# Attention and two feed-forward layers on one core: the first batch's values summed by TensorE, the second batch's queries and keys summed by GpSimd

## The chip, the cores and the metric

The kernel runs on one core of a Trainium2 chip. The metric is device time in microseconds (us) of one execution. TensorE is PE in the rows below (PEld its weight loads), VectorE is DVE, ScalarE is ACT, GpSimd is POOL, and SyncE is SP, which issues most of the DMAs.

## The reference

Four batches, eight heads, 576 tokens, 64 numbers per head. Two attentions are added: one over tokens averaged by fours (the pooled one, 144 queries and keys), its result repeated four times, and one over a narrow band of each token's neighbours (the local one). The 2304 tokens of 512 numbers that come out pass through two feed-forward layers, each 512 to 2048 to 512.

```python
def reference_core(q, k, v, w_in, w_out, w2_in, w2_out):
    q_d, k_d, v_d = (x.reshape(B, H, S // 4, 4, D).mean(axis=3) for x in (q, k, v))
    out_up = np.repeat(sm_attn(q_d, k_d, v_d), 4, axis=2)
    mask = np.abs(pos[:, None] - pos[None, :]) < 4
    scores = np.where(mask, scale * np.matmul(q, k.transpose(0, 1, 3, 2)), -1e9)
    out_local = np.matmul(softmax(scores), v)
    x = (out_up + out_local).transpose(0, 2, 1, 3).reshape(B * S, H * D)
    h = np.maximum(x @ w_in, 0.0)
    x = h * h @ w_out
    h = x @ w2_in
    g = np.maximum(h, 0.0) + np.log1p(np.exp(-np.abs(h)))
    return g @ w2_out
```

## The kernel before

**Order.** The program is written out by a planner. Each piece of work is a Python generator that yields the engine it wants, an assumed duration and what it needs; `Order.run` always takes the piece that could start first (ties by urgency) and only then emits its instructions. The planner's assumptions (for DMA those of `landed`) thus fix the order in which every engine runs its instructions; on the chip each engine works through its own list and waits in place for what is late.

**Feed-forward.** The tokens stand in five blocks of 512, 384, 512, 512 and 384 (`BLOCKS`). A step is one block times one of 16 slices of a layer: `hidden` makes `ph` with 12 products (each f32 product is split in a high and a low part, three products for each of four slices of the input), `activate` turns it into `gh` and `gl` on ScalarE and VectorE, and `outputs` adds 12 (or 9) products to `y`. The first two slices of the first block are done in halves of 256 tokens, so the first step needs only four of the eight local blocks (`half_ready`). Weights come as 64-bit numbers in half slices of 512 KB (`load_weights`, tile `raw`, three buffers) and are split on ScalarE and VectorE (`weight_job`: `f`, `r`, `w`).

**Attention of the first two blocks.** `pooled` handles one pair of heads: it sums queries and keys by fours (`qkd`), multiplies them (`psc`), takes the softmax (`pn`, `pe`), transposes it (`ppp`, copied to `ppt`), sums the values by fours (`vd`) and multiplies (`ppo`, copied to `up`). `local` handles 64 tokens: `lsc`, softmax in `le`, transpose `lpp`, copied to `lpt`, product with the values `lav`, to which `up` is added in `lt`; then the high part `xh` and the low part `xl` are the input of the feed-forward layer. For batch 0 VectorE makes both sums by fours; for batch 1 (`SUMS_ON_PE`) TensorE sums queries and keys with four products by the identity (`pqk`), and ScalarE copies the sum. Where TensorE's list would leave it idle before the fifth step, `keep_busy` puts in a product by the identity, `idle`, whose result nobody reads. The first pair tiles are lent from the weight slots and are called `w_first` in the rows; those of the values are called `first`.

**Loads.** SyncE's list goes, at the start, through identity, batch 0's queries and keys, its values (`pv`, 72 rows of 4 KB each), the mask, the local values (`lv`, 70 rows), the first two pairs of batch 1, and then the first weights.

Of the kernel before, what the change touches and what calls it, by code (L numbers as in the profile page):

```python
# [9 lines left out]
F32 = mybir.dt.float32  # L10
# [62 lines left out]
SUMS_ON_PE = [1]  # L73
# [17 lines left out]
CROWDED = 25.0  # L91
# [108 lines left out]
class Order:  # L200
# [85 lines left out]
def fused_kernel(ctx: ExitStack, tc: tile.TileContext, lq, lk, lv, dqk, dv, cdmask, pqk, pv, wts, cmask, cident, out):  # L286
# [13 lines left out]
    ident = const.tile([128, 128], F32, name="ident")  # L300
    mask = const.tile([128, 3, KW], F32, name="mask")
# [17 lines left out]
    r_pt = ring(att, "pt", [KH, 2 * 288], BUFS["pt"])  # L319
# [59 lines left out]
    more_slots = Event()  # L379
# [99 lines left out]
    lent, first_bufs = {}, {}  # L479

    def lend():

        for p in range(LENT):
            k = SLOTS1 - 1 - p
            lent[k] = Host()
            both = wpool.tile([128, 2048], F32, name=f"w_first{k}", tag=f"w{k}")
            if p < NP:
                first_bufs["in", p] = Guest(both[:, :2 * QKW], lent[k])
                first_bufs["in", p].left = 1 + BLOCKS[0]
                s0 = 2 * QKW  # L490
                first_bufs["qkd", p] = Guest(both[:, s0:s0 + 2 * SP], lent[k])
# [4 lines left out]
        for p, r in enumerate((r_xh[1], r_xl[1])):  # L496
            b = r.take("first")
            host = Host(b)
            x = b.tile.bitcast(F32).rearrange("p h n -> p (h n)")
            for two in range(2):  # L500
                first_bufs["pv", 2 * p + two] = Guest(x[:KH, two * 1024:two * 1024 + 1024], host)
# [26 lines left out]
    def load_tasks():  # L528
# [3 lines left out]
        order.landed(t, 65536)  # L532
# [5 lines left out]
        for (kind, at, hp, i, _), ev in zip(tasks, arrived, strict=True):  # L538
            if kind == "d":
                continue  # L540
            if kind == "l" and not i:
                if at % 2 == 0:
                    t = yield "sp", 0.06, *room(r_v, "v", at // 2)
                    bv = take_for(r_v, "v", at // 2)
                    bv.left = 2
                    sp.dma_start(out=bv.tile[:KW], in_=lv[at // 2])
                    vthere = order.landed(t, KW * 4096)
                ev.buf = None, None, bv, at % 2
                ev.at = 0.0
                ev.v.at = vthere  # L550
            elif kind == "l":
                if at % 2 == 0:
                    two = at // 2
                    t = yield "sp", 0.06, *room(r_q, "q", two), *room(r_k, "k", two), *room(r_v, "v", two)
                    bq, bk, bv = (take_for(r, x, two) for r, x in ((r_q, "q"), (r_k, "k"), (r_v, "v")))
                    for x in (bq, bk, bv):
                        x.left = 2
                    sp.dma_start(out=bq.tile, in_=lq[at // 2])
                    order.landed(t, 256 << 10)
# [5 lines left out]
                    vthere = order.landed(t, KW * 4096)  # L565
                ev.buf = bq, bk, bv, at % 2
                ev.at = there
                ev.v.at = vthere
            else:
                for x, two in [(ev, at * NP + hp)] + [(ev.next, at * NP + hp + 1)] * (at in BY_TWOS):  # L570
                    if at:
                        t = yield "sp", 0.06, r_in
                        x.buf = r_in.take("in")
                        sp.dma_start(out=x.buf.tile, in_=pqk[two])
                        x.at = order.landed(t, 128 * 8 * QKW)
                    late = i in DIRECT
# [4 lines left out]
                    x.v.at = order.landed(t, KH * 4096)  # L581
# [18 lines left out]
    def pooled(b, hp, banks, ev, pace):  # L600

        on_pe = b in SUMS_ON_PE
# [8 lines left out]
        if on_pe:  # L611
            t = yield "pe", 1.95, ev, pace, banks, r_s, r_e, r_n
            sums = bank(banks, "pqk")
            x4 = halves().rearrange("p a (j g) -> p a j g", j=FCT)
            src = sums.tile[:, :2 * SP].rearrange("p (a g) -> p a g", a=2)
# [6 lines left out]
            sums.free = t  # L622
# [36 lines left out]
        for a in range(2):  # L659
# [5 lines left out]
            for i in range(3):  # L665
                pe.transpose(pp.tile[:KH, i * 128:(i + 1) * 128], e3[:, i, a * KH:(a + 1) * KH], ident)
# [3 lines left out]
            used = pp.tile[:KH, :3 * (176 - RUN)].rearrange("p (i x) -> p i x", i=3)  # L670
            used = used[:, :, :128].rearrange("p i (h q) -> p i h q", h=2)[:, :, :, :48]
            copy(pt3[:, a, :].rearrange("p (i h q) -> p i h q", i=3, h=2), used)
            pp.free = t
        t = yield "dve", t_dve(1024), ev.v, r_vd
        vd = r_vd.take("vd")
        v4 = ev.v.tile.rearrange("p (i e j) -> p i e j", i=2, j=FCT)
        dve.tensor_reduce(out=vd.tile, in_=v4, axis=AX.X, op=ALU.add)
        ev.v.buf.free = t
        t = yield "pe", 0.66, banks
        po = bank(banks, "ppo")  # L680
        for a in range(2):
            pt4 = pt3[:, a, :].rearrange("p (i h q) -> p h i q", i=3, h=2)
            for h in range(2):
                pe.matmul(po.tile[64 * h:64 * h + 64, :SP], vd.tile[:, a, 64 * h:64 * h + 64], pt4[:, h],
                          start=(a == 0), stop=(a == 1))
        vd.free = pt.free = t
        t = yield either, t_either(144)
# [8 lines left out]
    def pooled_twos(b, hp, banks, ev, pace):  # L696
# [49 lines left out]
        for w in range(2):  # L746
            t = yield "pe", 0.66, Two(banks), r_pt
            pts.append(r_pt.take("ppt"))
            pt3 = pts[-1].tile.rearrange("p (a k) -> p a k", a=2)
# [13 lines left out]
        for w, (pt, vd) in enumerate(zip(pts, vds)):  # L763
            for h in range(2):
                for a in range(2):
                    pt4 = pt.tile.rearrange("p (a k) -> p a k", a=2)[:, a].rearrange("p (i h q) -> p h i q", i=3, h=2)
# [18 lines left out]
    def local(g, banks, ev, pace):  # L785
# [50 lines left out]
        for h in range(NP):  # L836
            for a in range(2):
                v0, q0 = (at * NP + h) * 128 + a * 64, h * 128 + a * QB
                pe.matmul(av.tile[a * 64:a * 64 + 64, h * QB:(h + 1) * QB], bv.tile[:KW, v0:v0 + 64],
                          pt.tile[:KW, q0:q0 + QB], start=True, stop=True)  # L840
# [5 lines left out]
        t = yield "dve", t_dve(256), up_ready[b]  # L846
        dve.tensor_tensor(out=o4, in0=av.tile[:, :NP * QB].rearrange("p (h g j) -> p h g j", h=NP, j=FCT),
                          in1=u4.to_broadcast([128, NP, QB // FCT, FCT]), op=ALU.add)
        av.free = t
# [3 lines left out]
        t = yield either, t_either(256, True), x_tiles[i]  # L853
# [4 lines left out]
        o.free = t  # L858
        left[i] -= 1
# [274 lines left out]
    with tc.manual_schedule():  # L1134
# [3 lines left out]
        order.spawn(load_weights(), 0, 8.0)  # L1138
# [11 lines left out]
        order.spawn(load_direct(), 0)  # L1150
        order.spawn(open_direct(), 0)
# [8 lines left out]
def _layout(q, k, v, moe_w_in, moe_w_out, moe2_w_in, moe2_w_out):  # L1160
# [24 lines left out]
    for b in SUMS_ON_PE:  # L1185
# [4 lines left out]
    pv = pv.transpose(0, 1, 4, 3, 2, 6, 5).reshape(B * NP, KH, 1024)  # L1190
    ws = []
# [16 lines left out]
    def inward(a):  # L1208
# [14 lines left out]
        "dqk": dqk, "dv": dv, "cdmask": dmask, "pqk": pqk, "pv": pv, "wts": np.ascontiguousarray(np.concatenate(ws, axis=0)).view(np.uint64),  # L1223
# [17 lines left out]
```

## Time and profile before

| | |
|---|---|
| time, median of 3 runs | 896.6 us (895.24 to 897.03) |
| the profiled execution's own time | 897.16 us |
| its span, first to last instruction | 895.4 us |
| TensorE busy | 884.2 us, 99% of the span |
| VectorE busy | 623.6 us, 70% |
| ScalarE busy | 482.6 us, 54% |
| GpSimd busy | 70.0 us, 8% |
| granted TensorE clock, mean | 1.00 |

The span is read together with the 1.76 us of the execution that lie around it. A busy engine need not do useful work: the `idle` products count as busy too. Shares of busy time are means over a span whose stages differ.

### The profile page before, as it was taken

To read this page: it belongs to the slowest core of one execution; us is meant where nothing else is said; L and a number is where in the kernel's file an instruction comes from. 1 tells how busy PE (TensorE), PEld (TensorE's weight loads), DVE (VectorE), ACT (ScalarE), POOL (GpSimd) and SP (SyncE) were. 2 spreads that over 40 slices of the span, in tenths; PEclk is the share of its full clock that TensorE was granted. 3 is DMA by queue.
4 is the path that set the end of the run, shared out by engine and by line. 5 is a ranking of instruction groups with operands and counts; after the bars stand their busy time and mean duration, and the time that the engine had idled before them with its cause. 6 is when DMAs were issued, how large, how long until landed. Compare 5 with 4: busy or idle time off the path is not lost.

```text
span 895.4 us, 13254 instructions
## 1 busy us (share of the span) xinstructions
PE 884.2 (99%) x4908; PEld 763.5 (85%) x4908; DVE 623.6 (70%) x1085; ACT 482.6 (54%) x1051; POOL 70.0 (8%) x136
## 2 busy tenths in 40 slices
PE   8999999999999999999999999999999999999998
PEld 7788899988888788888888888888999888988886
DVE  6999989999999999887888999982111224223222
ACT  4978877757767774552345543532333235444443
POOL 0000000000000000211111111111120110010000
PEclk9999999999999999999999999999999999999999
DMA  9599698859686854796866677636360262223001
GB/s 238 159 320 328 247 356 287 295 167 321 220 260 207 289 197 165 260 296 235 269 216 191 221 269 260 213 101 240 131 222 25 70 209 74 71 94 130 23 1 48
DMA packets 48796, 177.39 MB, mean 198 GB/s; under 512 B 5490, under 2 KB 5874, under 8 KB 48732
## 3 DMA queue, kind: packets, MB, share of 16 engines
q1 hardware_dynamic: 29724, 107.33, 35.7%
q0 software_dynamic: 19008, 69.21, 23.9%
q8 instruction: 39, 0.64, 0.3%
q14 instruction: 25, 0.20, 0.1%
HBM read 138.25 MB, written 38.27 MB: 197 GB/s over the span
## 4 chain that ended last, share of the span: by engine, by line
PE 78%; DVE 10%; DMA 6%; ACT 3%; issue 1%; SPq 0%; ACTq 0%; DVEq 0%
PE y L1069 38%; PE ph L1015 37%; DMA raw<-wts 3%; DMA w_first<-lv 1%; DVE gl L351 1%; DVE f L414 1%; DVE prod L935 1%; DVE f L410 1%; DVE w L351 1%; DVE dsc L906 1%; DMA in<-pqk 1%; DVE g L1038 1%; DVE do L942 1%; ACT f L401 1%; DMA w_first<-pqk 1%
## 5 line engine op out<-in xcount | busy, mean ns | idle before, releaser
L1015 PE MATMUL ph<-xh,w 128*128 128x512 f32 (+2 forms) x1304 | 393.8, 365 | 1.1 <-DVE g L1038 0.9
L1015 PEld LDWEIGHTS ph<-xh,w 128*128 128x128 f32 x1304 | 240.9, 188 | 32.9 <-DVE g L1038 1.8
L1015 PE MATMUL ph<-xl,w 128*128 128x512 f32 (+2 forms) x652 | 237.5, 364 | 0.0
L1069 PE MATMUL y<-gh,w 128*128 128x512 f32 (+2 forms) x656 | 199.6, 366 | 0.0
L1069 PE MATMUL y<-w,gh 128*128 128x512 f32 x576 | 179.2, 392 | 1.0 <-ACT o L338 1.0
L351 DVE TENSOR_TENSOR gl<-g,gh 128x512 fp32r<-128x512 f32 (+2 forms) x163 | 101.8, 625 | 85.3 <-ACT gh L338 84.5
L1015 PEld LDWEIGHTS ph<-xl,w 128*128 128x128 f32 x652 | 122.5, 188 | 15.6
L1069 PEld LDWEIGHTS y<-gh,w 128*128 128x128 f32 x656 | 121.0, 188 | 15.8 <-issue 1.2
L445 POOL DMA_DIRECT2D w<-wdram x132 | 69.8, 532 | 758.9 <-ACT gh L338 351.3
L1069 PEld LDWEIGHTS y<-w,gh 128*128 128x128 f32 x576 | 106.8, 188 | 22.4 <-ACT o L338 1.3
L1069 PE MATMUL y<-gl,w 128*128 128x512 f32 (+2 forms) x328 | 119.3, 364 | 0.0
L338 ACT ACTIVATE gh<-g 128x512 fp32r<-128x512 f32 (+2 forms) x127 | 72.9, 574 | 84.5 <-PE y L1069 49.6
L1038 DVE SCALAR_TENSOR_TENSOR g<-ph,g 128x512 f32<-128x512 f32 (+2 forms) x81 | 50.7, 626 | 90.6 <-ACT g L1036 90.4
L1069 PE MATMUL y<-w,gl 128*128 128x512 f32 x288 | 112.6, 391 | 0.0
L1027 ACT ACTIVATE g<-ph 128x512 f32<-128x512 f32 (+2 forms) x82 | 44.6, 543 | 122.8 <-PE ph L1015 102.9
L1032 ACT ACTIVATE g<-ph 128x512 f32<-128x512 f32 (+2 forms) x81 | 44.4, 548 | 100.8 <-PE ph L1015 91.7
L1069 PEld LDWEIGHTS y<-gl,w 128*128 128x128 f32 x328 | 61.6, 188 | 7.0 <-DVE gl L351 0.2
L1069 PEld LDWEIGHTS y<-w,gl 128*128 128x128 f32 x288 | 54.0, 188 | 11.7
L340 DVE CAST gh<-g 128x512 fp32r<-128x512 f32 (+2 forms) x36 | 14.9, 413 | 62.7 <-PE y L1069 51.8
L401 ACT ACTIVATE f<-raw 128x512 f32<-128x512 f32 x64 | 42.7, 671 | 19.0 <-DMA raw<-wts 8.2
L1030 ACT ACTIVATE g<-g 128x512 f32<-128x512 f32 (+2 forms) x82 | 47.5, 579 | 2.0
L1036 ACT ACTIVATE g<-g 128x512 f32<-128x512 f32 (+2 forms) x81 | 47.3, 584 | 2.2
(115 smaller groups left out, 926.6 us busy)
## 6 DMA issues: line engine op xcount, KB each, us to landing
w<-wdram POOLq DMA_DIRECT2D x132, 512.0 KB, 4.3
raw<-wts SPq DMA_DIRECT2D x64, 512.0 KB
wdram<-w SPq DMA_DIRECT2D x64, 512.0 KB
dqk<-dqk SPq DMA_DIRECT2D x11, 896.0 KB
dv<-dv SPq DMA_DIRECT2D x11, 640.0 KB
in<-pqk SPq DMA_DIRECT2D x12, 579.0 KB
out<-o SPq DMA_DIRECT2D x18, 256.0 KB
pv<-pv SPq DMA_DIRECT2D x12, 288.0 KB
```

What stands on the lines that cost most here:

```text
L338: act.activation(out=out, in_=in_, func=AF.Copy)
L340: dve.tensor_copy(out=out, in_=in_)
L351: dve.tensor_tensor(out=out, in0=whole, in1=high.bitcast(F32), op=ALU.subtract)
L401: act.activation(out=f.tile, in_=high.bitcast(F32), func=AF.Abs, scale=REBIAS)
L445: nc.gpsimd.dma_start(out=weights[slot][:, half], in_=wdram[c, half])
L1015: pe.matmul(ph.tile[:, :n], w, y, start=(k == 0), stop=(k == len(prs) - 1))
L1027: act.activation(out=o, in_=h, func=AF.Relu)
L1030: act.activation(out=o, in_=o, func=AF.Square)
L1032: act.activation(out=o, in_=h, func=AF.Abs)
L1036: act.activation(out=o, in_=o, func=AF.Ln, bias=1.0)
L1038: dve.scalar_tensor_tensor(out=o, in0=h, scalar=0.0, in1=o, op0=ALU.max, op1=ALU.add)
L1069: pe.matmul(o, wt, y, start=(begin and k == 0), stop=(end and k == 2))
```

## The change

The values of batch 0 are loaded as they stand, 128 tokens to a group, 512 numbers (all heads) to a token: four full groups in one DMA of 128 rows, the last 64 tokens in another. `sum_first` sums them by fours for all heads at once: four products by `placed`, a strip of zeros around 32 columns that add rows by fours, give 128 sums in one bank, a fifth gives the last 16. The keys of batch 0 are then split as 128 and 16 (before, 72 and 72), and `ppo` reads the sums from `first`. The queries and keys of batch 1 are summed by GpSimd (`ON_POOL`): an addition of 576 columns, then one of 288, in place of `pqk` and its copy. In the eight local blocks of the first feed-forward block, `up` is added to `lav` by TensorE (a product by the identity) and `xh` and `xl` read that bank; `lt` is no longer written there. The first three weight loads are issued before the loads of batch 1 (`begun`), and the planner's DMA rates are other numbers.

```diff
-SUMS_ON_PE = [1]
+ON_POOL = [1]
-CROWDED = 25.0
+RATE, FEWER = 3.3e5, 2.0e5
...
-    def landed(self, start, size):
+    def landed(self, start, size, rate=RATE):
         self.issue = max(self.issue, start) + 0.475
-        self.dma = max(self.dma, self.issue + 1.2) + size / (2.4e5 if self.dma < CROWDED else 3.3e5)
+        self.dma = max(self.dma, self.issue + 1.2) + size / rate
...
+            if j == jobs[RAWS - 1]:
+                begun.at = t
...
+    def sum_first():
+
+        tokens, sums = (x.tile for x in first_vd.parts)
+        nc.gpsimd.memset(placed, 0.0)
+        t = yield "dve", 0.2, first_v.ident
+        dve.tensor_reduce(out=fours, in_=ident.rearrange("p (g j) -> p g j", j=FCT), axis=AX.X, op=ALU.add)
+        t = yield "dve", 0.1
+        dve.tensor_copy(out=placed[:, 96:128], in_=fours)
+        t = yield "pe", 4.5, first_v, Two(every)
+        main, rests = bank(every, "pvm"), bank(every, "pvr")
+        for k in range(4):
+            pe.matmul(main.tile, placed[:, 96 - 32 * k:224 - 32 * k], tokens[:, k * 512:k * 512 + 512],
+                      start=(k == 0), stop=(k == 3))
+        pe.matmul(rests.tile[:16], fours[:64, :16], sums[:64, :512], start=True, stop=True)
+        first_vd.parts[0].free = t
+        t = yield either, t_either(512)
+        copy(sums[:, 512:1024], main.tile)
+        main.free = t
+        t = yield either, t_either(512)
+        copy(sums[:16, 1024:1536], rests.tile[:16])
+        rests.free = first_vd.at = t
...
+            if i and not begun.at:
+                yield None, 0.0, begun
...
+                        sp.dma_start(out=tokens, in_=pvn[:, :2048])
+                        order.landed(t, 1 << 20)
+                        t = yield "sp", 0.06
+                        sp.dma_start(out=sums[:64, :512], in_=pvn[:64, 2048:])
+                        first_v.at = order.landed(t, 128 << 10, FEWER)
...
-        if on_pe:
-            t = yield "pe", 1.95, ev, pace, banks, r_s, r_e, r_n
-            sums = bank(banks, "pqk")
...
-            for k in range(FCT):
-                pe.matmul(src, ident, x4[:, :, k], start=(k == 0), stop=(k == FCT - 1))
+        if on_pool:
+            t = yield "pool", 1.4, ev, pace
+            x4 = halves()
+            nc.gpsimd.tensor_tensor(out=x4[:, :, :2 * SP], in0=x4[:, :, :2 * SP], in1=x4[:, :, 2 * SP:], op=ALU.add)
+            t = yield "pool", 0.8, r_s, r_e, r_n
             qk, e, n = r_s.take("qkd"), r_e.take("pe"), r_n.take("pn")
+            nc.gpsimd.tensor_tensor(out=qk.tile.rearrange("p (a g) -> p a g", a=2), in0=x4[:, :, :SP],
+                                    in1=x4[:, :, SP:2 * SP], op=ALU.add)
             ev.buf.free = t
-            t = yield either, t_either(288)
-            copy(qk.tile, sums.tile[:, :2 * SP])
...
+        else:
+            t = yield "pe", 0.45, up_ready[b]
+            pe.matmul(av.tile[:, :NP * QB], ident, u4.to_broadcast([128, NP, QB // FCT, FCT]), start=False, stop=True)
+            o3 = av.tile[:, :NP * QB].rearrange("p (h q) -> p h q", h=NP)
...
-        order.spawn(load_weights(), 0, 8.0)
+        order.spawn(load_weights(), 0, 6.0)
```

The order of the emitted instructions moves with it. SyncE's list from the last pair of batch 0's queries and keys on was, before (`w_first` the lent tiles, `first` the values, `in` and `pv` batch 1, `raw` weights):

```order
L536 DMA w_first_86<-pqk 128x1158
L580 DMA first<-pv 72x1024
L584 DMA mask<-cmask 128x210
L580 DMA first<-pv 72x1024 x3
L546 DMA w_first_87<-lv 70x1024 x2
L546 DMA v<-lv 70x1024 x2
L574 DMA in<-pqk 128x1158
L580 DMA pv<-pv 72x1024
L574 DMA in<-pqk 128x1158
L390 DMA raw<-wts 128x1024 x4
```

and is now:

```order
L562 DMA w_first_88<-pqk 128x1158
L609 DMA first<-pvn 128x2048
L612 DMA first<-pvn 64x512
L623 DMA mask<-cmask 128x210
L574 DMA w_first_89<-lv 70x1024 x2
L574 DMA v<-lv 70x1024 x2
L392 DMA raw<-wts 128x1024 x3
L602 DMA in<-pqk 128x1158
L619 DMA pv<-pv 72x1024
L602 DMA in<-pqk 128x1158
L392 DMA raw<-wts 128x1024
```

Four loads of values have become two, and three weight loads stand ahead of batch 1's first pair.

On TensorE, the last stretch before the first feed-forward product (`ph`) was, before:

```order
L638 MATMUL psc<-qkd 64x144 x6
L839 MATMUL lav<-lpt,v 64x64 x8
...
L981 MATMUL idle<-ident 128x128 x7
L829 MATMUL lpp<-ident,le 70x128 x4
L981 MATMUL idle<-ident 128x128 x3
L839 MATMUL lav<-lpt,v 64x64 x8
...
L1015 MATMUL ph<-xh,w_78 128x256
```

and is now:

```order
L674 MATMUL psc<-qkd 64x144 x6
...
L886 MATMUL lav<-lpt,v 64x64 x8
L674 MATMUL psc<-qkd 64x144 x6
L900 MATMUL lav<-up,ident 128x256
L1069 MATMUL ph<-xh,w_80 128x256
```

The idle products have gone from this place, two pairs of batch 1 have their `psc` before the first `ph` instead of one, and local work (`lpp`, `lav`) that stood ahead of it comes behind it. In the whole list 49 `idle` products stood ahead of the first `ph` and 54 in all; now it is 24 and 44, of which 12, before 13, stand ahead of the first `psc`.

Behind the first `ph`, TensorE's list for batch 1 went on, before:

```order
L666 MATMUL ppp<-ident,pe 72x128 x3
L617 MATMUL pqk<-in,ident 128x288 x8
L684 MATMUL ppo<-ppt,vd 64x144 x4
L638 MATMUL psc<-qkd 64x144 x12
L1069 MATMUL y_864<-gh,w_78 128x256
```

The sums are now in GpSimd's list, four times, ahead of all of its DMAs:

```order
L490 MEMSET placed 128x224
L653 ISA
L653 TENSOR_TENSOR in<-in 128x2x288
L656 TENSOR_TENSOR qkd<-in 128x288
...
L449 DMA w_1570<-wdram 128x1024
```

The 16 `pqk` products and four copies by ScalarE are gone, and eight additions stand on an engine that had none. Which of VectorE and ScalarE makes a copy or a cast is the planner's choice too: VectorE's list has 7 `lpt` copies (before 3), 46 casts to `gh` (36), 23 casts to `w` (29) and 3 casts to `xh` from the first block's bank or `lt` (none).

## Rows read from the trace of the kernel before

**Rows 1.** The page: busy time of each engine, share of the span, instructions.
```profile
PE 884.2 (99%) x4908; PEld 763.5 (85%) x4908; DVE 623.6 (70%) x1085; ACT 482.6 (54%) x1051; POOL 70.0 (8%) x136
```

**Rows 2.** TensorE's waits over the span: us in total, times, longest.
```profile
PE idle L981 <- DMA ident<-cident: 2.6, 1, 2.6
PE y L1069 <- ACT o L338: 1.0, 1, 1.0
PE psc L638 <- ACT qkd L338: 1.0, 1, 1.0
PE ph L1015 <- DVE g L1038: 0.9, 1, 0.9
PE lpp L829 <- DVE pn L645: 0.4, 1, 0.4
PE lav L839 <- DVE lpt L340: 0.3, 1, 0.3
PE lav L839 <- ACT lpt L338: 0.3, 1, 0.3
```

**Rows 3.** Windows: us, busy time (instructions) by engine, clock, DMA share, GB/s.
```profile
5.00:45.00 40.00, 38.85 (x487) 32.46 (x486) 36.01 (x98) 30.54 (x131) 0.00 (x0) 1.00 0.73 201
200.00:260.00 60.00, 59.05 (x313) 50.76 (x312) 59.84 (x112) 44.90 (x95) 0.00 (x0) 1.00 0.78 265
600.00:889.00 289.00, 289.00 (x1416) 256.20 (x1416) 74.59 (x130) 115.15 (x210) 28.50 (x54) 1.00 0.31 101
```

**Rows 4.** TensorE's timeline, 0 to 60 us: start, us, instruction, wait ahead.
```profile
2.56 5.92 PE L981 MATMUL idle<-ident 128*128 128x128 f32 x26 [2.56 <-DMA ident<-cident]
8.41 0.98 PE L638 MATMUL psc<-w_first 64*64 64x144 f32 x12
...
30.61 2.10 PE L617 MATMUL pqk<-in,ident 128*128 128x288 f32 x8
32.64 1.15 PE L839 MATMUL lav<-lpt,w_first 70*64 70x64 f32 x32
...
37.71 1.83 PE L981 MATMUL idle<-ident 128*128 128x128 f32 x14
...
44.71 0.39 PE L1015 MATMUL ph<-xh,w 128*128 128x256 f32 x1
```

**Rows 5.** VectorE's timeline just before the first `ph`.
```profile
43.19 0.67 DVE L351 TENSOR_TENSOR w<-f,w 128x512 fp32r<-128x512 f32 x1
43.77 0.42 DVE L351 TENSOR_TENSOR xl<-lt,xh 128x256 fp32r<-128x256 f32 x1
```

**Rows 6.** VectorE's groups by shape, 0 to 113 us: busy us, mean ns, idle before.
```profile
L351 DVE TENSOR_TENSOR w<-f,w 128x512 fp32r<-128x512 f32 x16 | 10.9, 682 | 0.4 <-ACT w L338 0.4
...
L847 DVE TENSOR_TENSOR lt<-lav,up 128x256 f32<-128x256 f32 x14 | 5.8, 418 | 3.0 <-PE lav L839 2.8
...
L627 DVE TENSOR_REDUCE w_first<-w_first 128x288 f32<-128x1152 f32 x4 | 5.4, 1348 | 5.3 <-DMA w_first<-pqk 5.2
...
L677 DVE TENSOR_REDUCE vd<-first 72x256 f32<-72x1024 f32 x4 | 4.8, 1200 | 0.0
...
L340 DVE CAST w<-f 128x512 fp32r<-128x512 f32 x9 | 3.8, 419 | 0.0
...
L340 DVE COPY lpt<-lpp 70x512 f32<-70x512 f32 x3 | 2.0, 681 | 0.4 <-ACT le L816 0.4
```

**Rows 7.** Windows in the first loads, columns as in rows 3.
```profile
4.00:8.00 4.00, 4.00 (x20) 4.00 (x20) 2.71 (x2) 0.00 (x0) 0.00 (x0) 1.00 0.99 400
12.00:16.00 4.00, 3.95 (x68) 3.13 (x66) 4.00 (x12) 2.57 (x13) 0.00 (x0) 1.00 0.99 200
28.00:32.00 4.00, 3.99 (x30) 3.33 (x31) 3.79 (x13) 2.99 (x12) 0.00 (x0) 1.00 0.75 289
```

**Rows 8.** ScalarE's timeline: the first weights taken up.
```profile
31.73 0.66 ACT L401 ACTIVATE f<-raw 128x512 f32<-128x512 f32 x1
32.62 0.69 ACT L401 ACTIVATE f<-raw 128x512 f32<-128x512 f32 x1 [0.23 <-DMA raw<-wts]
```

More of the change, by code (lines that the diff above doesn't have):

```diff
@@ L495, in lend @@
                     first_bufs["v", two] = Guest(both[:KH, two * 1024:two * 1024 + 1024], lent[k])
[L496 to L501, printed above, removed]
+        x = [r.take("first") for r in (r_xh[1], r_xl[1])]
+        tokens, sums = (b.tile.bitcast(F32).rearrange("p h n -> p (h n)") for b in x)
+        first_vd.parts = Guest(tokens, Host(x[0])), Guest(sums, Host(x[1]))
+        first_vd.left = NP
     def take_for(r, kind, at):
@@ L531, in load_tasks @@
         sp.dma_start(out=ident, in_=cident)
-        order.landed(t, 65536)
+        first_v.ident.at = order.landed(t, 65536)
         for p, ev in enumerate(first_pairs):
@@ L546, in load_tasks @@
                     sp.dma_start(out=bv.tile[:KW], in_=lv[at // 2])
-                    vthere = order.landed(t, KW * 4096)
+                    vthere = order.landed(t, KW * 4096, FEWER)
                 ev.buf = None, None, bv, at % 2
@@ L564, in load_tasks @@
                     sp.dma_start(out=bv.tile[:KW], in_=lv[at // 2])
-                    vthere = order.landed(t, KW * 4096)
+                    vthere = order.landed(t, KW * 4096, FEWER)
                 ev.buf = bq, bk, bv, at % 2
@@ L575, in load_tasks @@
                         x.at = order.landed(t, 128 * 8 * QKW)
+                    if not at:
+                        if two:
+                            continue
+                        t = yield "sp", 0.06
+                        tokens, sums = (y.tile for y in first_vd.parts)
+                        sp.dma_start(out=tokens, in_=pvn[:, :2048])
+                        order.landed(t, 1 << 20)
+                        t = yield "sp", 0.06
+                        sp.dma_start(out=sums[:64, :512], in_=pvn[:64, 2048:])
+                        first_v.at = order.landed(t, 128 << 10, FEWER)
+                        continue
                     late = i in DIRECT
@@ L580, in load_tasks @@
                     sp.dma_start(out=x.v.tile, in_=pv[two])
-                    x.v.at = order.landed(t, KH * 4096)
+                    x.v.at = order.landed(t, KH * 4096, FEWER)
                 if todo:
@@ L658, in pooled @@
         n.free = t
-        for a in range(2):
+        keys = [(a * KH, KH) for a in range(2)] if b else [(0, 128), (128, SP - 128)]
+        for a, (k0, kn) in enumerate(keys):
             t = yield ("pe", 0.33, banks, r_pt) if a == 0 else ("pe", 0.33, banks)
@@ L669, in pooled @@
             t = yield either, t_either(288)
-            used = pp.tile[:KH, :3 * (176 - RUN)].rearrange("p (i x) -> p i x", i=3)
+            used = pp.tile[:kn, :3 * (176 - RUN)].rearrange("p (i x) -> p i x", i=3)
             used = used[:, :, :128].rearrange("p i (h q) -> p i h q", h=2)[:, :, :, :48]
-            copy(pt3[:, a, :].rearrange("p (i h q) -> p i h q", i=3, h=2), used)
+            copy(pt3[:kn, a, :].rearrange("p (i h q) -> p i h q", i=3, h=2), used)
             pp.free = t
[L674 to L678, printed above, removed]
+        if b:
+            t = yield "dve", t_dve(1024), ev.v, r_vd
+            vd = r_vd.take("vd")
+            v4 = ev.v.tile.rearrange("p (i e j) -> p i e j", i=2, j=FCT)
+            dve.tensor_reduce(out=vd.tile, in_=v4, axis=AX.X, op=ALU.add)
+            ev.v.buf.free = t
+            vds = [vd.tile[:, a] for a in range(2)]
+        else:
+            yield None, 0.0, first_vd
+            vd, (_, sums) = Event(), first_vd.parts
+            vds = [sums.tile[:kn, x + hp * 128:x + hp * 128 + 128] for x, (_, kn) in zip((512, 1024), keys)]
         t = yield "pe", 0.66, banks
         po = bank(banks, "ppo")
-        for a in range(2):
-            pt4 = pt3[:, a, :].rearrange("p (i h q) -> p h i q", i=3, h=2)
+        for a, (_, kn) in enumerate(keys):
+            pt4 = pt3[:kn, a, :].rearrange("p (i h q) -> p h i q", i=3, h=2)
             for h in range(2):
-                pe.matmul(po.tile[64 * h:64 * h + 64, :SP], vd.tile[:, a, 64 * h:64 * h + 64], pt4[:, h],
+                pe.matmul(po.tile[64 * h:64 * h + 64, :SP], vds[a][:, 64 * h:64 * h + 64], pt4[:, h],
                           start=(a == 0), stop=(a == 1))
         vd.free = pt.free = t
+        if not b:
+            first_vd.left -= 1
+            if not first_vd.left:
+                sums.free = t
         t = yield either, t_either(144)
@@ L858, in local @@
         o.free = t
+        if not i:
+            av.free = t
         left[i] -= 1
@@ L1150, in fused_kernel @@
         order.spawn(load_direct(), 0)
+        order.spawn(sum_first(), -1000)
         order.spawn(open_direct(), 0)
@@ L1184, in _layout @@
     pqk[:, :, 0, :S], pqk[:, :, 1, :S] = qt.reshape(B * NP, 128, S), kt.reshape(B * NP, 128, S)
-    for b in SUMS_ON_PE:
+    for b in ON_POOL:
         x = pqk[b * NP:(b + 1) * NP, :, :, :S]
@@ L1190, in _layout @@
     pv = pv.transpose(0, 1, 4, 3, 2, 6, 5).reshape(B * NP, KH, 1024)
+    pvn = np.zeros((5, 128, DM), f4)
+    pvn.reshape(-1, DM)[:S] = np.asarray(v, f4)[0].transpose(1, 0, 2).reshape(S, DM)
+    pvn = pvn.transpose(1, 0, 2).reshape(128, -1)
     ws = []
```

39 lines of the change are left out of this document (21 added, 18 removed).

## The prediction

> **What bounds the kernel now.** I read the page first. TensorE is busy for 884.2 of 895.4 us, the others far less [rows 1]. Next its waits: seven, 6.5 us together, of which 2.6 us stand ahead of the first instruction [rows 2]. So TensorE's list runs almost without a gap, and the time is the sum of what stands in that list, plus those waits and the tail behind the last product. But the list holds work that nobody reads: 54 `idle` products. The windows then show which other engine could set the pace. VectorE is busy for 36.0 of the 40 us from 5 to 45 us and for 59.8 of the 60 us from 200 to 260 us, but for only a quarter of the time behind 600 us [rows 3]. Inside the stretch from 200 to 260 us TensorE has its one wait for VectorE that carries weight, 0.9 us for `g` [rows 2]. So there are two accounts to keep: what leaves TensorE's list, and whether VectorE, up to about 260 us, comes forward by as much.
>
> **TensorE's list, term by term.** (a) The `pqk` products go. Four of them (eight records, since the trace shows each f32 product of this kind as two) begin at 30.61 us, and the next kind at 32.64 us [rows 4]: 2.03 us for a pair, 0.51 us for a product of 288 columns. Sixteen are 8.1 us.
> (b) `up` is added by a product of 256 columns in eight blocks. By columns from (a) that is 0.51 x 256/288 = 0.45 us, eight times 3.6 us.
> (c) The values' sums are five products of 512 columns: 0.51 x 512/288 = 0.90 us, together 4.5 us. That these go by columns, with a strip of zeros or a repeated operand, no row shows; if a repeated operand cost nothing or twice as much, (b) would be 0 or 7.2 us, and both ends are kept for the range. I take 3.6, since `pqk` reads a whole operand by the same identity.
> (d) `idle`. The first 13 took from 2.56 to 8.41 us, 0.45 us each; later seven took 1.83 us, 0.26 us each [rows 4]. The order has one fewer ahead of the first `psc` and nine fewer behind: 0.45 + 9 x 0.26 = 2.8 us.
> (e) TensorE's wait of 1.0 us for ScalarE's copy `qkd` [rows 2] has no copy to wait for any more.
> The splits 128 and 16 in place of 72 and 72 change nothing here: as many transposes and `ppo` products, with the same moving columns.
> Sum: -8.1 + 3.6 + 4.5 - 2.8 - 1.0 = -3.8 us.
>
> **What hides the rest.** Loads: rows of 128 partitions came in at 400 GB/s, the values and local values on 72 and 70 partitions at 200 [rows 7]. The values of batch 0 (4 x 288 KB) took some 6 us and now take some 3; the weights also pass 1.5 MB of batch 1. Adding up, first weights land near 20 us; before, ScalarE took them up at 31.7 us and waited for the second [rows 8]. By itself I price this at nothing, because the first `ph` needs two things that were ready within half a microsecond of each other: the weights' low part at 43.86 us and the last `xl` at 44.19 us, for a `ph` at 44.71 us [rows 4, 5]. It is the cover for TensorE's earlier start: without it, `ph` would stay at 44 us or so. With it, TensorE's list reaches `ph` at about 40.6 us: 25 fewer `idle` (0.45 + 24 x 0.26 = 6.7), no `pqk` (2.0), less local work ahead (about 3.0), but one more `psc` (0.9), the five sums (4.5) and five additions of `up` (2.3). That is work moved, not gained, and counts only through (a) to (e).
> Batch 1's first pair now lands behind three weights, near 25 us by the same rates, and its `psc` stands at 36 to 37 us in TensorE's list. GpSimd thus has some 11 us for a pair. No row shows an addition on GpSimd. From below, VectorE takes 0.68 us for a two-input instruction of 512 columns [rows 6], so 864 columns are at least 1.1 us; from above, anything up to the 11 us is hidden by the local work in between. I take 2.3 us, twice VectorE's, and a price on the path of nothing. Behind it on GpSimd stand only the reloads of weights, which began far later.
> [...]
>
> **VectorE.** It loses the four `vd` sums of batch 0 (4.8 us) and eight `lt` additions (8 x 0.42 = 3.3 us), 8.1 us in all [rows 6]. Given back by the new order: four more `lpt` copies (7 in place of 3, 2.7 us), the copy of the sums (0.7 us, as an `lpt` of 512 columns) and three casts to `xh` (1.3 us at `xl`'s 0.42): 3.4 us are left. Over the whole program it also gets ten more `gh` casts and six fewer `w` casts, a net 4 x 0.42 = 1.7 us [rows 6]. So by 260 us it is 1.7 to 3.4 us ahead; I take 2.5. TensorE's list is ahead by 3.8. In the stretch where VectorE has 0.2 us of slack in 60 [rows 3], the wait for `g` grows by the difference, 1.3 us. Behind 600 us VectorE is idle for most of the time, so nothing more is lost, but the 1.3 us do not come back.
>
> **The forecast.** -3.8 + 1.3 = -2.5 us. The profiled execution took 897.16 us, 1.76 more than its span; 897.16 - 2.5 = 894.7. It was 0.56 us above the median of 896.6, so against that: **894.1 us**. A measurement of this kernel can tell about 0.2%, 1.8 us, from no change.
>
> **The rivals.** *VectorE keeps up.* Its few idle moments between 5 and 200 us absorb the difference, and the waits for `g` (0.9) and for the bank that `o` frees (1.0) [rows 2] fall away too: -3.8 - 1.9 = -5.7, 890.9 us. For it: 4 us idle from 5 to 45 us [rows 3]. Against: both waits lie where the order has hardly changed.
> *The gain is given back in the first 110 us.* The removed `idle` products were the place where TensorE waited; if what it waited for comes no sooner, the 2.8 us of (d) return as waits, and what is left is -2.5 + 2.8 = +0.3: 896.9 us, no change. For it: VectorE was 90% busy from 5 to 45 us, and the order behind the first `ph` now holds more local work that passes through VectorE. Against: the weights land some 10 us earlier and VectorE has 8 us less to do.
> *GpSimd holds VectorE up (slower).* The eight additions fall in the stretch from 25 to 65 us, in which VectorE has little slack. If VectorE stands still while GpSimd reads, it loses at most 4 x 2.3 = 9 us (4.6 us if GpSimd is as fast as VectorE), and at least nothing. The point from which it decides: beyond 2.5 us VectorE is later than before everywhere up to 260 us, and each further microsecond lengthens the kernel; at 4.6 us lost that is +2.1 (898.7), at 9 us +6.5 (903.1). [...] Against: most of VectorE's instructions there read PSUM or one operand, and they would have to collide with nearly every addition.
>
> **Chances.** Forecast 0.50, VectorE keeps up 0.13, given back 0.25, GpSimd in the way 0.12. The first two are faster than 894.8 us, except for a part of the forecast's own spread (an error of 0.7 us in the VectorE account suffices), of which I move 0.06 to the middle; of the last, some 0.03 end within 0.2%. So faster 0.57, same 0.34, slower 0.09. The range reaches from the dense case to a little past the given-back one, 890.8 to 897.6 us; (b) at twice its price lies inside.
>
> **What would show it.** Right: first `ph` near 40.6 us; `pvm` in 0.9 us steps; no wait at the batch-1 `psc`; GpSimd's pairs well ahead of their `psc`; VectorE still full from 200 to 260 us and TensorE's wait for `g` at some 2 us; `idle` 20 records fewer. Wrong: new TensorE waits between 40 and 110 us (the second rival); VectorE's two-input instructions longer or late beside GpSimd's additions (the third); first weights taken up later than 25 us, so that the early start is not covered.

## The result, and the profile after

The changed kernel takes 904.25 us (median of 8 runs, 898.69 to 908.95), the kernel before 896.63 beside it: a ratio of 1.0086, 95% interval 1.0069 to 1.0103. It is slower by some 7.6 us. Of the 73 runs of before that were timed beside the experiments, 69 list a mean granted TensorE clock of 0.999 or 1.000 and four 0.995 to 0.998; the eight runs of the changed kernel list 0.990 to 0.999, and the slowest run has the lowest clock.

The profiled execution is the quickest of the eight (898.69 us, clock 0.999, span 896.9). That of `e1_again` below, the same kernel once more, took 901.35 us, the quickest of its six; so no profile shows the kernel at its median. The page's row, against [rows 1]:

```profile
PE 882.9 (98%) x4882; PEld 759.4 (85%) x4882; DVE 631.6 (70%) x1093; ACT 474.8 (53%) x1030; POOL 80.3 (9%) x145
```

TensorE's waits over the span (us in total, times, longest), against [rows 2]:

```profile
PE idle L1035 <- DMA ident<-cident: 2.7, 1, 2.7
PE lav L886 <- DVE lpt L342: 2.1, 2, 1.6
PE ph L1069 <- DVE g L1092: 1.9, 2, 1.4
PE dpp L1003 <- DVE do L996: 0.4, 1, 0.4
```

The waits for `qkd` and for the bank that `o` frees are gone; the longest wait for `lpt`, 0.3 us before, is 1.6, and the waits for `g` have grown from 0.9 to 1.9 us in all. TensorE's timeline shows the new work at its forecast length, and the wait:

```profile
16.14 3.60 PE L498 MATMUL pvm<-first,placed 128*128 128x512 f32 x8
19.67 1.03 PE L500 MATMUL pvr<-first,fours 64*16 64x512 f32 x2
20.63 0.60 PE L703 MATMUL ppp<-ident,w_first 128*16 128x128 f32 x4
...
30.56 0.60 PE L900 MATMUL lav<-up,ident 128*128 128x256 f32 x2
31.00 0.60 PE L876 MATMUL lpp<-ident,le 128*70 128x128 f32 x4
31.43 0.39 PE L1035 MATMUL idle<-ident 128*128 128x128 f32 x2
33.38 0.69 PE L886 MATMUL lav<-lpt,w_first 70*64 70x64 f32 x16 [1.56 <-DVE lpt L342]
```

From start to start, four `pvm` are 3.53 us and `pvr` 0.96; one addition of `up` is 0.44. What makes `lpt` late stands in GpSimd's timeline and VectorE's beside it:

```profile
26.72 1.41 POOL L653 TENSOR_TENSOR in<-in 128x576 f32<-128x576 f32 x1 [25.70 <-ACT ppt L340]
28.22 0.87 POOL L656 TENSOR_TENSOR qkd<-in 128x288 f32<-128x288 f32 x1
29.52 1.72 POOL L653 TENSOR_TENSOR in<-in 128x576 f32<-128x576 f32 x1 [0.44 <-DMA in<-pqk]
31.32 1.12 POOL L656 TENSOR_TENSOR qkd<-in 128x288 f32<-128x288 f32 x1
```

```profile
27.54 1.83 DVE L411 TENSOR_SCALAR f<-f 128x512 uint32<-128x512 uint32 x2
29.29 0.68 DVE L414 SCALAR_TENSOR_TENSOR f<-raw,f 128x512 uint32<-128x512 uint32 x1
29.89 0.44 DVE L853 SCALAR_TENSOR_TENSOR ls<-lsc,mask 128x280 f32<-128x280 f32 x1
30.25 1.54 DVE L418 CUSTOM_DVE_ANT_0 f<-f,r 128x1024 uint16<-128x1024 uint16 x1
...
32.07 0.66 DVE L342 CAST w<-f 128x512 fp32r<-128x512 f32 x1
32.65 0.68 DVE L342 COPY lpt<-lpp 70x512 f32<-70x512 f32 x1
```

GpSimd does a pair in 2.4 us, as forecast. But while it adds, VectorE's instructions on `f` are stretched: two `f<-f` take 1.83 us, the custom one (`CUSTOM_DVE_ANT_0`) 1.54. What they take without the additions is shown under `e5_pool_short`.

### The profile page after: what moved, and what is told of

It is laid out like the page before. It is cut to its first block, busy times and chain, and to the rows that moved or that the text cites. A ratio compares the mean times of both kernels' runs of the same rounds, so it can differ in the third digit from the quotient of the medians.

```text
span 896.9 us, 13185 instructions
## 1 busy us (share of the span) xinstructions
PE 882.9 (98%) x4882; PEld 759.4 (85%) x4882; DVE 631.6 (70%) x1093; ACT 474.8 (53%) x1030; POOL 80.3 (9%) x145
## 4 chain that ended last, share of the span: by engine, by line
PE 82%; DVE 12%; DMA 2%; issue 2%; ACT 1%; ACTq 0%; DVEq 0%
PE ph L1069 39%; PE y L1123 38%; DMA raw<-wts 1%; DVE f L414 1%; DVE f L418 1%; DVE w L353 1%; DVE do L996 1%; DVE prod L989 1%; DVE gl L353 1%; PE idle L1035 1%; PE psc L767 1%; DVE dsc L960 1%; DVE prod L953 1%; DVE f L411 1%; PE lsc L848 1%
## 5 line engine op out<-in xcount | busy, mean ns | idle before, releaser
L340 ACT ACTIVATE gh<-g 128x384 fp32r<-128x384 f32 (+2 forms) x117 | 66.4, 567 | 89.6 <-PE y L1123 60.4
L342 DVE CAST gh<-g 128x512 fp32r<-128x512 f32 (+2 forms) x46 | 19.1, 415 | 66.1 <-PE y L1123 59.3
```

Of the source, the lines that this page charges most:

```text
L340: act.activation(out=out, in_=in_, func=AF.Copy)
L342: dve.tensor_copy(out=out, in_=in_)
```

## The experiments

Each was timed against the kernel before on the same chip, in five rounds: e1 to e4, e5 to e8 and e9 to e12 on a chip each, so across these groups the ratios are what to compare. The last column has the mean granted clock of the kernel's runs.

| | median us (lowest to highest) | ratio to before, 95% | clock |
|---|---|---|---|
| e1_again | 903.94 (901.35 to 907.28) | 1.0084 (1.0065 to 1.0103) | .993 to .997 |
| e2_fill | 903.87 (900.79 to 908.07) | 1.0080 (1.0060 to 1.0101) | .992 to 1.000 |
| e3_pqk_on_pe | 898.82 (898.61 to 899.82) | 1.0022 (1.0012 to 1.0032) | .999 to 1.000 |
| e4_vd_on_dve | 900.88 (899.36 to 902.18) | 1.0044 (1.0031 to 1.0057) | .995 to .998 |
| e5_pool_short | 897.85 (896.29 to 900.22) | 1.0011 (0.9998 to 1.0025) | .996 to .999 |
| e6_fill_more | 903.50 (902.39 to 904.58) | 1.0073 (1.0057 to 1.0090) | .997 to 1.000 |
| e7_values_no_up | 898.18 (897.54 to 898.96) | 1.0012 (1.0001 to 1.0023) | .997 to 1.000 |
| e8_early_only | 897.99 (896.97 to 899.73) | 1.0012 (0.9998 to 1.0025) | .999 to 1.000 |
| e9_short_fill_g | 896.57 (894.62 to 898.67) | 1.0002 (0.9991 to 1.0012) | .998 to 1.000 |
| e10_fill_all | 900.27 (899.90 to 900.77) | 1.0042 (1.0030 to 1.0055) | .999 to 1.000 |
| e11_two_pairs_pool | 897.91 (897.07 to 899.55) | 1.0019 (1.0010 to 1.0028) | .999 to 1.000 |
| e12_values_two_pairs | 895.69 (894.40 to 900.66) | 0.9991 (0.9974 to 1.0007) | .996 to 1.000 |

**The changed kernel once more** (no edit).

> The changed kernel once more, for the stretch in which its typical execution differs from the profiled one (898.7 us at a mean granted clock of 0.999, where seven others took 902.7 to 909.0 us at 0.990 to 0.997). Theory A: TensorE falls to the lower clock level for some 10 us in a typical execution, right behind the wait of 1.6 us near 32 us; times again 898 to 909 us, and if this profile's mean clock is 0.997 or lower, its windows show the low clock between 30 and 50 us. Theory B: the low clock lies elsewhere, in the tail or behind the first 113 us; then the early windows show 1.00. Theory C: the time differs for another reason (loads, VectorE), and windows with the clock at 1.00 all along are longer.

The `lav` waits again, 2.31 us now. What follows is in TensorE's timeline, and in the windows (us, busy time of PE, PEld, DVE, ACT and POOL, clock, DMA share, GB/s):

```profile
33.19 0.69 PE L886 MATMUL lav<-lpt,w_first 70*64 70x64 f32 x16 [2.31 <-DVE lpt L342]
33.80 1.03 PE L876 MATMUL lpp<-ident,le 128*70 128x128 f32 x4
...
38.42 0.60 PE L876 MATMUL lpp<-ident,le 128*70 128x128 f32 x4
```

```profile
32.00:36.00 4.00, 2.81 (x29) 2.00 (x30) 3.73 (x9) 2.51 (x11) 0.26 (x1) 0.74 0.23 93
36.00:40.00 4.00, 4.00 (x64) 3.56 (x64) 3.69 (x9) 3.34 (x10) 0.00 (x0) 0.84 0.94 274
40.00:44.00 4.00, 4.00 (x64) 3.61 (x59) 3.28 (x9) 2.57 (x15) 0.00 (x0) 1.00 0.68 226
```

After the wait four transposes take 1.03 us, at 38.42 us the same four 0.60, and the two windows show a mean clock of 0.74 and 0.84: TensorE runs at a lower clock behind the wait, as theory A has it. If that clock is the 0.50 of two windows of `e2_fill` below, the means make an estimated 2.1 + 1.3 = 3.4 us of it, from about 33.9 to 37.3 us. At the third pair of batch 1 the roles are changed: one of GpSimd's additions lasts 3.65 us, and a `psc` waits 1.3 us for it.

**Work put into the first wait.**

```diff
+FILL = {1: 6}
...
+        for _ in range(FILL.get(g, 0)):
+            pe.matmul(av.tile[:, :128], ident, ident, start=True, stop=True)
```

> The changed kernel with six products by the identity put ahead of the second local block's product with the values, into the bank that it will overwrite; the order is otherwise the same. In the profiled execution TensorE stood there 1.6 us waiting for a copy by VectorE, and six products are as long. Theory A (the low clock begins with this wait, because TensorE stands still): all executions at a mean clock of 0.999 or more, 895 to 899 us. Theory B or C: spread and median as in the changed kernel run beside it, 904 us.

The clock stays at 1.00 from 32 to 40 us, but the time is the one expected of B and C: the profiled execution, the slowest of the six (908.07 us), loses more at the third pair. Rows of GpSimd, TensorE and the windows there:

```profile
54.05 5.51 POOL L654 TENSOR_TENSOR in<-in 128x576 f32<-128x576 f32 x1 [21.69 <-DMA in<-pqk]
59.64 0.79 POOL L657 TENSOR_TENSOR qkd<-in 128x288 f32<-128x288 f32 x1
```

```profile
60.48 1.71 PE L675 MATMUL psc<-qkd 64*64 64x144 f32 x12 [2.80 <-POOL qkd L657]
```

```profile
60.00:64.00 4.00, 3.52 (x21) 3.01 (x22) 1.76 (x4) 0.78 (x3) 0.43 (x1) 0.50 0.33 107
64.00:68.00 4.00, 3.94 (x27) 3.12 (x26) 2.50 (x9) 2.33 (x9) 0.00 (x0) 0.50 0.91 292
68.00:72.00 4.00, 4.00 (x29) 4.00 (x29) 4.00 (x7) 2.49 (x7) 1.88 (x2) 0.79 1.01 296
```

An addition that took 1.41 us elsewhere takes 5.51 here, TensorE stands still for 2.80 us, and then runs for 8 us at a clock of 0.50 and for part of four more (mean 0.79; in the windows the clock is the third number from the end). So the place can move; the pair of events, a wait and then the low clock, is the same.

**GpSimd's part undone** (`pqk` and its copy again, order planned anew).

```diff
-            nc.gpsimd.tensor_tensor(out=x4[:, :, :2 * SP], in0=x4[:, :, :2 * SP], in1=x4[:, :, 2 * SP:], op=ALU.add)
+                pe.matmul(src, ident, x4[:, :, k], start=(k == 0), stop=(k == FCT - 1))
```

> GpSimd's part undone: batch 1's queries and keys are summed by TensorE again, the rest of the change stays, planned anew. [...] Rival (the thinned list of TensorE alone brings the clock down): 902 us or more with clocks below 0.997.

The clock is back at 0.999 or more, where the rival has it below 0.997, and the runs lie within 1.2 us of each other. The time, 898.82 us, is some 2 us above before. By the list that is no surprise: with `pqk` back, the values' sums (4.5) and `up` (3.6) add 8.1 us, of which 17 fewer `idle` products give back some 4.6. Whether that is all of it was not tested.

**The values' part undone, GpSimd's kept** (`vd` on VectorE).

> The values' part undone: batch 0's values are loaded by pairs of heads and summed by VectorE again; GpSimd's sums, the early weights and the addition of up on TensorE stay, planned anew (57 idle products). If GpSimd's collisions are at the root: VectorE instructions of 1.5 us and more beside GpSimd's additions again, and a time above 898 us. If the five products for the values and the narrower splits that go with them are at the root: mean clock 0.999, 895 to 898 us.

Still slower and still at a lower clock: a wait of 2.1 us for `lpt`, then 0.57 from 36 to 40 us. Here ScalarE makes that copy; it stands behind an instruction that waits 2.0 us for VectorE, whose `f<-f` takes 1.64 and whose custom instruction 1.28 us beside the additions. GpSimd's part does harm without the values' part too.

**GpSimd's additions made short, everything else in the changed kernel's order** (the cut shows the first of the two additions; `psc` reads unsummed numbers).

```diff
-            nc.gpsimd.tensor_tensor(out=x4[:, :, :2 * SP], in0=x4[:, :, :2 * SP], in1=x4[:, :, 2 * SP:], op=ALU.add)
+            nc.gpsimd.tensor_tensor(out=x4[:, :, :4], in0=x4[:, :, :4], in1=x4[:, :, 2 * SP:2 * SP + 4], op=ALU.add)
```

> The changed kernel in its own order on every engine, but GpSimd's eight additions cover 8 columns each, and psc of the second batch reads a quarter of the loaded queries and keys unsummed (so the second batch's pooled attention is left out of the computation; TensorE's products have the same sizes). Theory (GpSimd's long additions and VectorE's instructions hold each other up, TensorE stands still for it near 32 and 58 us, and its granted clock falls afterwards): the waits for lpt and qkd are under 0.5 us, VectorE's instructions beside the additions keep their usual length, the granted clock is 0.999 or more in all runs, their times lie within 1.5 us of each other, and the time is 893 to 897 us, as the prediction's sum of the list gives. Rival (the new order itself, with VectorE's lpt copy on the path and five sums ahead of it, makes the waits and the clock): 901 to 905 us, granted clock 0.993 to 0.997.

This gives back 6 us (904 to 897.85; the ratio falls from 1.0084 to 1.0011). VectorE's same instructions now, and the wait for `lpt` is 0.6 us:

```profile
27.43 0.75 DVE L411 TENSOR_SCALAR f<-f 128x512 uint32<-128x512 uint32 x2
...
29.07 0.68 DVE L418 CUSTOM_DVE_ANT_0 f<-f,r 128x1024 uint16<-128x1024 uint16 x1
...
30.02 0.42 DVE L342 CAST w<-f 128x512 fp32r<-128x512 f32 x1
30.72 0.69 DVE L342 COPY lpt<-lpp 70x512 f32<-70x512 f32 x1 [0.28 <-PE lpp L880]
```

1.08 + 0.86 + 0.24 = 2.2 us were lost to the long additions on these three rows alone. Three things were not as expected: the spread is 4 us (6.4 in the 29 runs of before beside it), the clock goes down to 0.996, and the time is above the expected 893 to 897 us. TensorE's timeline near 254 us shows a part of this:

```profile
251.51 0.33 PE L1073 MATMUL ph<-xl,w 128*128 128x384 f32 x1
251.69 0.34 PE L1073 MATMUL ph<-xh,w 128*128 128x384 f32 x1
253.93 0.51 PE L1073 MATMUL ph<-xh,w 128*128 128x384 f32 x1 [1.90 <-DVE g L1096]
254.24 0.52 PE L1073 MATMUL ph<-xl,w 128*128 128x384 f32 x1
254.56 0.84 PE L1073 MATMUL ph<-xh,w 128*128 128x384 f32 x2
```

TensorE was 1.45 us ahead of before at 113 us, but `g` came only 0.5 us sooner. This `ph` stood, in the kernel before, at 254.44 us:

```profile
254.44 0.44 PE L1015 MATMUL ph<-xh,w 128*128 128x384 f32 x1 [0.94 <-DVE g L1038]
```

The wait is 1.90 us in place of 0.94 [rows 2], and the products behind it are 0.32 us apart, before it 0.17; the mean clock is 0.77 from 252 to 256 us and 0.80 from 256 to 260. At the next `psc`, at 273.55 us against 272.54, the lead has become a lag of 1.0 us.

**Work in the waits for `lpt` and ahead of the last two pairs' `psc`** (6 and twice 10 products by the identity, as in `e2_fill`).

> The changed kernel with 6 products by the identity, which nobody reads, ahead of the second local block's lav, and 10 ahead of each of the last two psc of the second batch; GpSimd's sums stay. 26 x 0.26 = 6.8 us of work, of which what TensorE would have waited for costs nothing. Theory (the loss beyond the waits is the clock, which falls after TensorE has stood still): granted clock 0.999 or more in nearly all runs, narrow spread, 899 to 902 us in spite of the added work. Rival (the clock falls for another reason, with GpSimd's work or in single executions): clocks 0.990 to 0.997 again, and 906 to 910 us.

The spread is 2.2 us in place of `e1_again`'s 5.9 and the clock is higher, but the time is 1.5 us above the expected range: the fourth pair's products covered no wait (10 x 0.26 = 2.6 us of plain work), and the wait for `g` was not filled. Neither theory fits alone; `e10_fill_all` changes both.

**Parts of the change without GpSimd**: `e7_values_no_up` (values' sums, early weights, rates) and `e8_early_only` (early weights, rates).

> The change with two parts undone: the second batch's sums are TensorE's again, and up is added by VectorE again; the values' sums on TensorE, the early weights and the rates stay. TensorE's list by the products' lengths is 0.2 us shorter than before's. Theory (without GpSimd the time is the sum of the list): 895.5 to 898 us, granted clock 0.999 or more. Rival (the values' sums or the early weights cost more than their columns): 899 us or more.

> Only the early first weights and the planner's rates are left of the change. TensorE's list is 0.8 us shorter than before's (51 idle products). Theory (the earlier weights alone are worth what they take from idle): 895 to 897 us, granted clock 0.999 or more. Rival (VectorE is the bound ahead of the first ph, and the gain comes back as a wait): 896.5 to 898 us.

Each comes out within 0.2% of before, and each above its theory's range; `e8_early_only` lies where its rival had it, so 51 idle products in place of 54 were not worth their 0.8 us. `e7_values_no_up`, which has no additions on GpSimd, lists 0.997 in five of eleven runs: in its profiled execution a wait of 1.2 us for `xh` near 118 us is followed by a clock of 0.57 from 120 to 124 us.

**The wait for `g` filled**, GpSimd's additions short.

```diff
+FILL_PH = {40: 3}
...
+            if s in FILL_PH:
+                for name in ("fill0", "fill1"):
+                    spare = r_a.make(name)
+                    for _ in range(FILL_PH[s]):
+                        pe.matmul(spare[:, :128], ident, ident, start=True, stop=True)
```

> The kernel with GpSimd's additions of 8 columns (the second batch's sums left out, as in that run), and 6 products by the identity, which nobody reads, put into the two attention banks ahead of the one hidden product that waits 1.9 us for g near 254 us; the order is otherwise the same on every engine. Theory (TensorE's granted clock falls behind a wait, and that is what is left of the loss): the products fit into the wait, cost nothing, the clock stays at 0.999 or more in all runs, the spread narrows, 895.5 to 897.5 us. Rival (the clock falls there for another reason): clocks 0.996 to 0.999 as before and 897.5 to 899.5 us.

At the same place there is no wait of weight left (0.3 us for `g`) and no low clock (1.00 from 252 to 260 us):

```profile
251.32 1.50 PE L1071 MATMUL fill<-ident 128*128 128x128 f32 x12
252.57 0.42 PE L1080 MATMUL ph<-xh,w 128*128 128x384 f32 x1
252.83 0.33 PE L1080 MATMUL ph<-xl,w 128*128 128x384 f32 x1
253.00 0.51 PE L1080 MATMUL ph<-xh,w 128*128 128x384 f32 x2
```

The runs do not tell that this saves time: the ratio to before is 1.0002 in place of 1.0011, the intervals overlap, the spread is 4 us as in `e5_pool_short`, and four of twelve runs still list 0.998.

**All three waits filled, GpSimd's additions at full length.**

> The changed kernel with its full additions on GpSimd, and unread products by the identity at the three places where TensorE waits: 6 ahead of the second local block's lav, 10 ahead of the third pair's psc of the second batch, 6 ahead of the hidden product that waits for g. 22 x 0.26 = 5.7 us of work, less the waits that they cover. Theory: granted clock 0.999 or more in all runs, 899 to 902 us, below the changed kernel without them. Rival (the clock follows GpSimd's work and not the waits): 0.993 to 0.997, 905 us or more.

This decides on the clock: it follows TensorE's waits, not GpSimd's work. It is 0.999 or 1.000 in all six runs, 0.993 to 0.997 in those of `e1_again`. GpSimd does all that it does in the changed kernel (the third pair's first addition lasts 5.19 us here too), TensorE has 5.7 us more to do, and the kernel is some 4 us quicker than the changed one (1.0042 against 1.0084 of before), with every run between 899.9 and 900.8 us. The windows of the first two places:

```profile
32.00:36.00 4.00, 3.29 (x49) 2.70 (x49) 4.00 (x11) 2.85 (x12) 0.01 (x1) 1.00 0.43 131
56.00:60.00 4.00, 3.78 (x34) 3.25 (x33) 1.96 (x5) 0.93 (x2) 3.92 (x2) 1.00 0.55 169
60.00:64.00 4.00, 3.85 (x45) 3.39 (x46) 2.85 (x7) 2.12 (x8) 0.10 (x1) 1.00 0.47 178
```

**Only the last two pairs on GpSimd**: `e11_two_pairs_pool` is otherwise the kernel before, `e12_values_two_pairs` has the values' sums and early weights as well, without the product that adds `up`.

```diff
+POOL_PAIRS = [6, 7]
-        if on_pool:
+        if on_pool and two not in POOL_PAIRS:
```

> The kernel before, with the sums of only the last two pairs of the second batch on GpSimd (the additions then stand near 54 and 68 us); nothing else of the change. TensorE's list is 3.6 us shorter than before's. Theory (the additions and VectorE hold each other up wherever they meet, and VectorE sets the pace near 254 us): the 3.6 us come back as waits and as lower clock, 896 to 900 us. Rival (only the first two pairs, ahead of the first hidden product, do harm): 893 to 895 us.

> The change without the product that adds up, and with the first two pairs' sums on TensorE: values' sums on TensorE, early weights, only the last two pairs on GpSimd. TensorE's list is 4.2 us shorter than before's, and VectorE has 4.8 us less to do. Theory (what GpSimd's additions take from VectorE fits into what the values' sums gave it): 893.5 to 896.5 us. Rival (the meeting of the two engines costs TensorE a wait near 58 us and the clock behind it): 897 to 901 us, granted clock 0.995 to 0.998.

`e11_two_pairs_pool` is no quicker for its list of 3.6 us less: new waits have come, among them 1.7 us for `pe` and 1.9 in all for `gl`, both from VectorE, though no lower clock. Rows of GpSimd, and VectorE's beside them:

```profile
47.71 1.41 POOL L655 TENSOR_TENSOR in<-in 128x576 f32<-128x576 f32 x1 [47.27 <-DVE w L354]
...
59.02 1.41 POOL L655 TENSOR_TENSOR in<-in 128x576 f32<-128x576 f32 x1 [8.69 <-DMA in<-pqk]
60.50 0.86 POOL L658 TENSOR_TENSOR qkd<-in 128x288 f32<-128x288 f32 x1
```

```profile
47.77 1.90 DVE L415 SCALAR_TENSOR_TENSOR f<-raw,f 128x512 uint32<-128x512 uint32 x1
49.59 1.02 DVE L354 TENSOR_TENSOR xl<-lt,xh 128x256 fp32r<-128x256 f32 x1
50.54 0.41 DVE L354 TENSOR_TENSOR gl<-g,gh 128x256 fp32r<-128x256 f32 x1
...
59.03 1.68 DVE L343 CAST w<-f 128x512 fp32r<-128x512 f32 x1
60.63 1.20 DVE L351 TENSOR_TENSOR pe<-pe,pn 128x432 f32<-128x432 f32 x1
```

So the harm is not confined to the first two pairs. `e12_values_two_pairs`, where VectorE has 4.8 us less to do, is the quickest kernel by its median, 895.69, but its interval against before holds 1: not told apart. Some of its runs list a clock of 0.996; what that costs it was not tested.

## Why the prediction was wrong

Forecast were 894.1 us and a range of 890.8 to 897.6; measured 904.25. Of the 10 us between them some 6 belong to GpSimd's additions at full length (904.1 against 897.85). The rest is there with short additions too, and is explained in part.

**TensorE's list: right.** The new products cost what (b) and (c) said: 0.44 and 0.88 to 0.96 us each, so repeated operands and strips of zeros go by columns here. `pqk` is gone and 44 idle products are left. With short additions and the `g` wait filled, the profiled execution's last product ends 2.6 us before that of the kernel before, but its span is only 1.4 us shorter, and the medians of `e9_short_fill_g` and before do not differ (1.0002). A place that the forecast took as unchanged is the tail: from the last product to the end of the span it is 4.3 us before, and 5.2 to 5.7 in the profiled executions of the changed kernel and of the six others with its order. What makes it longer was not traced. The first `ph` stands at 41.28 us, 39.54 with short additions; forecast 40.6. First weights are taken up at 25.09 us, before at 31.73 [rows 8].

**VectorE's account: mis-sized.** It was to be 2.5 us ahead by 260 us. With short additions it is 0.5 us ahead at `g`, with full ones 1.25 us behind (255.69 against 254.44). The account left out work that the planner moved to VectorE: two more `w_first<-w_first,pn` products (0.60 us each) and two more copies to `up` (0.31 each), 1.8 us. The mechanism was the forecast's, `g` setting TensorE's pace there and the wait growing by about 1 us (0.94 to 1.90 with short additions); the clock behind it, 0.77 and 0.80 in the windows there, was left out.

**The step that failed** is the price of GpSimd's sums, "a price on the path of nothing". The 2.3 us for a pair, an estimate from VectorE's rows, were right (26.72 to 29.09 us, 2.37), and the first pair had its 11 us of cover (its addition starts at 26.72 us, its `psc` at 38.11); but the cover is for GpSimd's own length, not for what it does to VectorE. The rival *GpSimd holds VectorE up* is what happened, and both arguments against it were wrong. That most of VectorE's instructions there read PSUM or one operand did not save it, and that such instructions are spared no row had shown: `f<-f` and the cast to `w`, with one operand each, were held up too (0.75 to 1.83 and 0.42 to 0.66 us). And the two need not collide with nearly every addition: one collision ahead of an `lpt` or a `psc` is enough to stop TensorE (for 1.56 us at the `lpt` of the changed kernel, 2.80 at the `psc` of `e2_fill`). Up to that `g` VectorE's 487 instructions, the same in both runs, take 4.7 us longer in sum than with short additions, near the rival's 4.6 us, and this profiled execution came out where the rival put it for that loss (898.69 against 898.7); the second is in part luck, since TensorE lost its time at `lpt` as well as at `g`.

The rival's price for the usual run was too low all the same, for two reasons. It let only VectorE lose, while GpSimd's additions also grew from 1.41 to 5.51 us, and it counted a wait at its length, while waits of 1.9 to 2.8 us were followed by an estimated 3.4 to 10 us at a clock of 0.50 (worked out from the means of the windows: 0.77 and 0.80 in `e5_pool_short`, 0.74 and 0.84 in `e1_again`, 0.93, 0.50, 0.50 and 0.79 in `e2_fill`), of which half is lost. Not every wait had that price: waits of 1.3 to 1.7 us in the profiles of the changed kernel, `e1_again`, `e2_fill` and `e6_fill_more` were followed by no low clock, the 1.2 us in `e7_values_no_up` were (0.57 from 120 to 124 us). What decides between them is not shown.

**How the 6 us divide.** Full additions against short: 904.1 to 897.85. The median of the runs' granted clocks is 0.995 against 0.9985; on 897 us that is an estimated 3 us from the clock, and by subtraction 3 are left for the waits and the late VectorE. It is a rough estimate: in the profiled execution of `e6_fill_more` (0.998) the only low clock stands behind the last product, where it costs nothing. `e10_fill_all` agrees with it: waits filled at a price of 5.7 us of work, and still 4 us less. How an execution falls on one side or the other of a collision, and with it the time between 898.7 and 909 us, was not traced further than that the additions do not meet the same instructions each time: the third pair's first addition starts at 52.35 us in one execution of the changed kernel and at 54.30 us in another.

## What to carry to other kernels

Work given to an engine that idles was not free here: GpSimd does a pair in 2.4 us, and its additions at full length cost the kernel some 6 us (904.1 against 897.85). Look at what VectorE runs at the same time, and test it with additions made short in an unchanged order. Where TensorE's clock falls behind a wait (to 0.50 for 8 us behind the 2.80 us in `e2_fill`), that wait costs its length plus half of the slow stretch; unread products in a wait that can't be removed may cost less than they save (5.7 us of them in `e10_fill_all`, and still 4 us less). And when a list gets shorter ahead of a stretch that another engine paces, expect the gain back as a wait there (for `g` 0.94 us before, 1.90 in `e5_pool_short`).

## What the runs showed of the hardware

Where GpSimd's additions and VectorE's instructions met in the rows below, one kept its length and the other was held. In `e11_two_pairs_pool` the addition at 59.02 us took its 1.41 us, and the cast to `w` that began 0.01 us later took 1.68 us in place of 0.41 and ended 0.28 us behind it. In `e5_pool_short` an addition of 8 columns, 0.20 us at 26.81 us with VectorE idle, lasted this long:

```profile
51.40 4.37 POOL L656 TENSOR_TENSOR qkd<-in 128x8 f32<-128x8 f32 x1
```

It ended at 55.77 us. VectorE, whose instructions kept their usual length meanwhile, had then just run out of work (its last one ended at 55.70). So it did in `e2_fill`: its last instruction ended at 58.30 us, and the addition that had begun at 54.05 ended 1.26 us later. Spans on GpSimd are rough in the profile, but TensorE's `psc`, which waits for this pair's sum, bears them out: it starts at 60.48 us, just behind the second addition's end at 60.43. A wait for one instruction would have been at most 1.2 us here, the longest of VectorE's in those 4.37 us: GpSimd was held over a whole run of them. Not every meeting does this: in the same run the addition of 8 columns at 29.89 us took 0.20 us beside a VectorE reduction (`ln<-ls`, 29.67 us, 0.44). What decides is not shown.
